# The last V pair of a cached-attention decode block, loaded in three pieces, its first piece partly by transfers of three partitions

## Chip, core and metric

One core of one Trainium2 chip runs the whole kernel. The metric is the device time of one execution in microseconds (us), lower is better. Before the change the median of three runs is 1293.55 us (1293.53 to 1293.67).

## What is computed

One decode step of a transformer block, in bf16: layer norm, attention of 4 sequences x 32 heads over a cache of 8192 keys and values, an output projection with residual, then a gated feed-forward part with its own layer norm and residual. The caches are 2 x 256 MiB, and each is read once.

```python
def _A_ref(x, k_cache, v_cache, wq, wo):          # x: [4, 1, 512], caches: [4, 32, 8192, 128]
    q = (x @ wq).reshape(B, Sq, H, Dh).transpose(0, 2, 1, 3)
    scores = jnp.einsum("bhqd,bhkd->bhqk", q, k_cache) * (Dh ** -0.5)
    p = _softmax(scores, axis=-1)
    o = jnp.einsum("bhqk,bhkd->bhqd", p, v_cache)
    return o.transpose(0, 2, 1, 3).reshape(B, Sq, H * Dh) @ wo
def _B_ref(x, w_gate, w_up, w_down):
    h = _sigmoid(x @ w_gate) * (x @ w_up)
    return h @ w_down
h  = x + _A_ref(_layernorm(x), k_cache, v_cache, wq, wo)
h2 = h + _B_ref(_layernorm(h), w_gate, w_up, w_down)
```

## The kernel before

The 128 (sequence, head) caches of K are handled in 64 pairs of heads, numbered n = 0 to 63, and those of V likewise. A pair is a tile of 128 partitions x 16384 bf16 values (32 KB in each partition, 4 MiB in all). It lies in one of the four slots of the SBUF tensor `KV`. Slots are handed out in rotation by `take_slot`; a transfer into a slot waits until the pair that held it before has been used up: a K pair by its last transpose on VectorE (line 380), a V pair by its last matmul (line 473).

All large transfers are issued by SyncE (SP) in one written order, `order` (line 333): the query weights, then K and V pairs alternately with K four pairs ahead, and at the end V60, V61, V62, V63, `wg`, `wu`, `wd` (gate, up and down weights, which go into slots of `KV` too). `wg` waits for the slot of V60, `wu` for that of V61, `wd` for that of V62. SP issues one after the other, so a transfer that waits for its slot holds back those behind it. A transfer over 128 partitions is carried by 16 DMA engines, each of which works through its rows in order of issue. `wd` comes as three transfers of 8, 4 and 2 of its 14 row blocks (`WDT`).

A pair is used in eight chunks of 4 KB per partition (`RC` x `DH` = 2048 values; `NCH` = 8). For V, `pv(u)` multiplies chunk m of pair n with the softmax weights in `PT`: four matmuls of 128x512 for each chunk. `t_v[n]` lists the completion tokens of the transfers that bring pair n, and `pv` waits for the one that covers its chunk. All V pairs come as one transfer, except the last one, V63: `emit_pair` cuts it into four transfers of two chunks each (1 MiB, 8 KB per partition; lines 297 to 301), with a semaphore each (`vl0` to `vl3`).

After the last chunk of V63 comes a chain of small steps: `finish` (copy to `O_sb`, selection matmuls of line 491, transposition of line 498, projection of line 507), the second layer norm (lines 207 to 225), the gate and up matmuls (line 596), the sigmoid (line 601), the product `hhT` (line 603), and the down matmuls (line 624), which need `hhT` and the three parts of `wd`. The cast of line 629 and the output transfer of line 630 end the kernel.

Of the kernel before, what the change touches and what calls it, by code (L numbers as in the profile page):

```python
# [11 lines left out]
NSL = 4  # L12
# [3 lines left out]
GH = 8  # L16
GP = 4
WDT = (0, 8, 12, 14)


class _Prog:
# [27 lines left out]
    def emit(self, eng, fn, waits=(), incs=1):  # L49

        todo = self._waits(eng, waits)
        tok = self.token(eng, incs) if incs else None

        def run(e):
            for key, v in todo:
                e.wait_ge(self.sems[key], v)
            made = fn(e)
            made = made if isinstance(made, list) else [made]
            if incs:
                assert len(made) == incs  # L60
                for m in made:
                    m.then_inc(self.sems[eng], 1)

        self.ops[eng].append(run)
        return tok
# [14 lines left out]
def bass_sequential_preLN__mha_block_cached__glu_gated_glu__decode_kernel(  # L80
# [13 lines left out]
    _, H, S, DH = A_k_cache.shape  # L94
# [5 lines left out]
    RC = 16  # L100
    NCH = R // RC
    NH = B * H
    NP = NH // 2
# [6 lines left out]
    prog = _Prog()  # L110
    emit = prog.emit

    with ExitStack() as es:
        def SB(name, shape, dt):
            return es.enter_context(nc.sbuf_tensor(name, shape, dt))
# [19 lines left out]
        KV = SB("KV", [128, NSL, R * 128], BF16)  # L135
# [28 lines left out]
        def in_slot(slot, inner, at=0):  # L164
            return bass.AP(raw(KV), slot * R * 128 + at, [[KVROW, 128], *inner])
# [10 lines left out]
        def obank(g):  # L176
            return bank[2 + g % 2]

        keys = ["sp", "act", "dve", "pool", "pe", "x", "out", "wg", "wu", "wd0", "wd1", "wd2", "wq", "wo"]
        keys += [f"sl{i}" for i in range(NSL)] + [f"k0p{i}" for i in range(4)] + [f"vl{i}" for i in range(4)]  # L180
        for k in keys:
            prog.sems[k] = es.enter_context(nc.semaphore("s_" + k))

# [3 lines left out]
            out=ident[:, :], in_=ident[:, :], compare_op=ALU.not_equal, fill=1.0, base=0,  # L187
# [3 lines left out]
            out=identf[:, :], in_=identf[:, :], compare_op=ALU.not_equal, fill=1.0, base=0,  # L191
# [74 lines left out]
        t_v = {}  # L266
# [4 lines left out]
        def kv_src(cache, n):  # L271
            b, h = n % GP, 2 * (n // GP)
            return cache[b, h:h + 2, :, :].rearrange("h (p r) d -> (h p) (r d)", p=64)
# [12 lines left out]
        def take_slot(job):  # L286
            i = n_alloc[0] % NSL
            w = freed(held_by[i])
            n_alloc[0] += 1
            held_by[i] = job  # L290
            slot_of[job] = i
            return i, w

        def emit_pair(kind, n, cache, done, pieces, cut):
            slot, w = take_slot((kind, n))
            src = kv_src(cache, n)
            if cut > 1:
                q = R * 128 // cut
                done[n] = [prog.dma("sp", f"{pieces}{s}", lambda e, s=s: e.dma_start(
                    KV[:, slot, q * s:q * (s + 1)], src[:, q * s:q * (s + 1)]), w) for s in range(cut)]  # L300
                return
            done[n] = [prog.dma("sp", f"sl{slot}", lambda e: e.dma_start(KV[:, slot, :], src), w)]

        def emit_weight(kind):
            slot, w = take_slot((kind, 0))
            if kind == "wd":
                wd_v = in_slot(slot, [[D, NFT], [1, D]])
                src = B_w_down.rearrange("(t p) f -> p t f", p=128)
                t_w[kind] = (wd_v, [prog.dma("sp", f"wd{i}", lambda e, i=i: e.dma_start(  # L309
                    wd_v[:, WDT[i]:WDT[i + 1], :], src[:, WDT[i]:WDT[i + 1], :]), w) for i in range(len(WDT) - 1)])  # L310
                return
            view = in_slot(slot, [[F, NDC], [1, F]])
            src = (B_w_gate if kind == "wg" else B_w_up).rearrange("(c p) f -> p c f", p=128)
            t_w[kind] = (view, prog.dma("sp", kind, lambda e: e.dma_start(view, src), w))

        def emit_wq():
            src = A_wq.rearrange("(p c) f -> p (c f)", p=128)
            t_wq.append(prog.dma("sp", "wq", lambda e: e.dma_start(Wreg[:, :], src)))
# [4 lines left out]
        def emit_wo():  # L323
            src = A_wo.rearrange("(g p e) f -> p g (e f)", p=128, e=4)
            dst = Wreg[:, :].rearrange("p (g f) -> p g f", g=NG // 2)
            t_wo.append(prog.dma("sp", "wo", lambda e: e.dma_start(dst, src), [t_qproj[0]]))  # L326
# [11 lines left out]
        def ready(kind, n):  # L338
            if kind == "wo":
                return bool(t_qproj)  # L340
            return kind == "wq" or freed(held_by[n_alloc[0] % NSL]) is not None

        def pump():
            while next_dma[0] < len(order) and ready(*order[next_dma[0]]):
                kind, n = order[next_dma[0]]
                next_dma[0] += 1
                if kind == "k":
                    emit_pair("k", n, A_k_cache, t_k, "k0p", 4 if n == 0 else 1)
                elif kind == "v":
                    emit_pair("v", n, A_v_cache, t_v, "vl", 4 if n == NP - 1 else 1)  # L350
                elif kind == "wq":
                    emit_wq()
                elif kind == "wo":
                    emit_wo()
                else:
                    emit_weight(kind)

        pump()


# [4 lines left out]
        t_ptc = {}  # L365
# [89 lines left out]
        def pv(u):  # L455
            n, m = u // NCH, u % NCH
            g, i = n // GP, n % GP
            first = i == 0 and m == 0
            last = i == GP - 1 and m == NCH - 1
            slot = slot_of["v", n]  # L460
            w = [t_v[n][m * len(t_v[n]) // NCH], t_ptc[g]]
            if first and g > 1:
                w.append(t_oev[g - 2])

            def f(e):
                mms = []
                for j in range(4):
                    k = 4 * m + j
                    o = k * 128 + i * 32
                    at = [[RC * 128, 4], [1, 128]], (64 * (k % 2) + k // 2) * 128  # L470
                    if n:
                        at = [[1, 512]], 512 * k
                    mms.append(e.matmul(obank(g)[32 * j:32 * (j + 1), :], PT[:, g % 2, o:o + 32], in_slot(slot, *at),  # L473
                                        start=first, stop=last, tile_position=(0, 32 * j)))
                return mms if last else mms[-1]
            tok = emit("pe", f, w, incs=4 if last else 1)
            if m == NCH - 1:
                t_pv[n] = tok
            if last:
                t_pvg[g] = tok  # L480
# [75 lines left out]

        q_projection()
        pump()
        for kind, n in steps:
            for m in range(NCH):  # L560
                u = NCH * n + m
                if kind == "k":
                    transposes(n, m)
                    advance()
                    scores(u)
                    if m == NCH - 1:
                        if n + NLQ < NP:
                            q_windows(n + NLQ)
                        if n % GP == GP - 1:
                            chain += [(tick[0] + d, fn) for d, fn in softmax(n // GP)]  # L570
                else:
                    advance()
                    pv(u)
                    if m == NCH - 1 and n % GP == GP - 1:
                        chain += [(tick[0] + d, fn) for d, fn in finish(n // GP)]
                pump()
# [10 lines left out]
        t_hn, _ = layernorm(sth, st_["h"], 1, hnT, bank[XS], st_["xs"])  # L587
# [30 lines left out]
        t_r = emit("pe", f_res, [t_res])  # L618
        for i in range(len(WDT) - 1):
            def f_down(e, i=i):  # L620
                mms = []
                for t in range(WDT[i], WDT[i + 1]):
                    for c in range(NDC):
                        mms.append(e.matmul(rows(c), hhT[:, t, :], wd_v[:, t, 128 * c:128 * (c + 1)],  # L624
                                            start=False, stop=(t == NFT - 1), tile_position=(0, 32 * c),
                                            skip_group_check=True))
                return mms[-4:]
# [5 lines left out]
        key, v = t_out  # L633
# [55 lines left out]
```

## Time and profile before

| what | value |
|---|---|
| median of three runs | 1293.55 us |
| the profiled execution's own time | 1293.53 us |
| its span, first to last instruction | 1291.7 us |
| TensorE matmul busy | 777.4 us (60%) |
| VectorE busy | 722.6 us (56%) |
| bytes read from HBM | 550.77 MB, 426 GB/s over the span |
| share of the ordinary DMA queue (q1) of 16 engines' span | 99.5% |
| mean granted TensorE clock | 0.790 |

The span leaves out 1.83 us of the profiled execution that lie before its first and after its last instruction. Matmul busy time is modelled at its end and says little of a limit; the DMA share is a mean over the 16 engines, so a share under 1 can mean that some of them have nothing left to do while others still work. A line of the timeline gives start and length of a group of instructions, the engine, the line of the program, the operation, the tiles it writes and reads, the number of instructions, and in brackets how long the engine had been idle before and what ended that.

### The profile page before, as it was taken

Reading aid. Unit: us, or ns where it says so; the run is one execution under the profiler, and the core shown is the slowest. Engines: PE = TensorE matmul, PEld = TensorE weight load, DVE = VectorE, ACT = ScalarE, POOL = GpSimd, SP = SyncE. Lnnn points to the kernel's source line nnn. Section 1 sums busy time; section 2 is a strip of 40 time slices with the busy share of each in tenths; the row PEclk is TensorE's granted clock in tenths of the full one; section 3 lists DMA queues with packets and bytes.
Section 4 is the critical chain, followed back from the end, with each engine's and each line's share of the span. In section 5 each row is a group of like instructions: output and inputs, shape, how many; then the busy total and the mean of one; then the engine's idle time right before and its main releaser. Section 6 shows DMA issues by size and latency. Waiting matters only on the chain.

```text
span 1291.7 us, 10570 instructions
## 1 busy us (share of the span) xinstructions
PE 777.4 (60%) x4768; PEld 308.4 (24%) x4768; DVE 722.6 (56%) x761; ACT 28.0 (2%) x56; POOL 10.9 (1%) x13
## 2 busy tenths in 40 slices
PE   4575656647557557556656657466465666566464
PEld 2222212213212222222222222122122222222122
DVE  5584745736555555645637556465645647456340
ACT  0000000000000000000000000000000000000001
POOL 3000000000000000000000000000000000000000
PEclk9788778877788687787788787787787886787775
DMA  9999999999999999999999999999999999999997
GB/s 396 430 432 428 435 428 434 429 431 431 433 431 428 433 431 432 428 433 432 432 430 431 432 430 434 427 435 429 430 435 426 435 428 433 434 425 437 425 433 305
DMA packets 23448, 551.45 MB, mean 427 GB/s; under 512 B 2280, under 2 KB 4076, under 8 KB 6124
## 3 DMA queue, kind: packets, MB, share of 16 engines
q1 hardware_dynamic: 23396, 550.78, 99.5%
q8 instruction: 37, 0.61, 0.2%
q14 instruction: 7, 0.06, 0.0%
q10 hardware_dynamic: 8, 0.00, 0.0%
HBM read 550.77 MB, written 0.00 MB: 426 GB/s over the span
## 4 chain that ended last, share of the span: by engine, by line
DMA 76%; DVE 21%; PE 1%; SPq 1%; issue 0%; ACT 0%
DMA KV<-in_A_k_cache_dram 72%; DVE kTc L380 21%; DMA KV<-in_A_v_cache_dram 2%; DMA Wreg<-in_A_wq_dram 1%; PE PS L399 1%; SPq L309 1%; DMA KV<-in_B_w_down_dram 1%; PE PS L521 0%; PE PS L473 0%; ACT E_sb L434 0%; DVE mpart L411 0%; PE PS L624 0%; PE PS L429 0%; SPq L326 0%; PE PS L440 0%
## 5 line engine op out<-in xcount | busy, mean ns | idle before, releaser
L399 PE MATMUL PS<-kTc,Lq 128*128 128x512 bf16 x2048 | 589.1, 446 | 450.7 <-DVE kTc L380 446.7
L380 DVE STREAM_TRANSPOSE kTc<-KV 128x1024 f32<-128x1024 f32 x512 | 586.8, 1209 | 371.2 <-DMA KV<-in_A_k_cache_dram 363.4
L399 PEld LDWEIGHTS PS<-kTc,Lq 128*128 128x128 bf16 x2048 | 210.0, 110 | 817.4 <-DVE kTc L380 545.9
L473 PE MATMUL PS<-KV,PT 128*32 128x512 bf16 x2048 | 138.0, 397 | 23.2 <-DMA KV<-in_A_v_cache_dram 14.3
L452 DVE STREAM_TRANSPOSE PT<-E_sb 64x512 bf16<-64x512 bf16 x32 | 78.4, 2450 | 1.0
L473 PEld LDWEIGHTS PS<-KV,PT 128*32 128x32 bf16 x2048 | 49.9, 99 | 85.5 <-issue 28.4
L545 DVE TENSOR_TENSOR Lq<-q,amask 128x16 bf16<-128x16 bf16 x64 | 14.2, 229 | 85.7 <-PE PS L399 85.6
L434 ACT ACTIVATE E_sb<-PS,negmb 128x512 bf16<-128x512 f32 x16 | 11.0, 687 | 1194.2 <-DVE negmb L432 1194.2
L491 PE MATMUL PS<-O_sb,pick 128*64 128x128 f32 x128 | 31.5, 428 | 0.8 <-ACT O_sb L483 0.8
L496 DVE CAST O_row<-PS 128x128 bf16<-128x128 f32 x8 | 2.3, 292 | 51.8 <-PE PS L491 51.8
L491 PEld LDWEIGHTS PS<-O_sb,pick 128*64 128x64 f32 x128 | 25.1, 224 | 13.8 <-issue 12.2
L416 PE MATMUL PS<-identf,mpart 128*1 128x128 f32 x32 | 6.1, 271 | 13.8 <-DVE mpart L411 13.8
L442 DVE RECIPROCAL rsum<-PS 128x1 f32<-128x1 f32 x16 | 2.7, 168 | 19.4 <-PE PS L440 19.3
L411 DVE TENSOR_REDUCE mpart<-PS 128x1 f32<-128x512 f32 x16 | 10.9, 684 | 2.1 <-PE PS L399 2.1
L579 POOL MEMSET kTc<- 128x448 bf16 x1 | 0.5, 471 | 1225.8 <-PE PS L399 1225.8
L483 ACT ACTIVATE O_sb<-PS 128x512 f32<-128x512 f32 x16 | 9.6, 597 | 53.8 <-PE PS L473 53.8
L521 PE MATMUL PS<-xnT,Wreg 128*128 128x4 bf16 x128 | 3.6, 166 | 8.6 <-DMA Wreg<-in_A_wq_dram 8.6
L440 PE MATMUL PS<-sig,Gmat 128*128 128x1 f32 x32 | 6.0, 257 | 4.5 <-ACT E_sb L434 4.5
L420 DVE TENSOR_REDUCE mrow<-PS 1x8 f32<-1x128 f32 x16 | 4.4, 276 | 7.1 <-PE PS L473 7.1
L429 PE MATMUL PS<-identf,rowpad 128*128 128x1 f32 x32 | 6.0, 257 | 2.8 <-DVE rowpad L424 2.8
L440 PEld LDWEIGHTS PS<-sig,Gmat 128*128 128x128 f32 x32 | 4.8, 187 | 12.1 <-ACT E_sb L434 11.9
L429 PEld LDWEIGHTS PS<-identf,rowpad 128*128 128x128 f32 x32 | 4.8, 187 | 10.4 <-DVE rowpad L424 10.3
(70 smaller groups left out, 75.8 us busy)
## 6 DMA issues: line engine op xcount, KB each, us to landing
KV<-in_A_k_cache_dram SPq DMA_DIRECT2D x63, 4096.0 KB, 29.7
KV<-in_A_v_cache_dram SPq DMA_DIRECT2D x63, 4096.0 KB, 34.9
Wreg<-in_A_wq_dram SPq DMA_DIRECT2D x1, 4096.0 KB, 12.2
KV<-in_A_k_cache_dram SPq DMA_DIRECT2D x4, 1024.0 KB, 17.9
Wreg<-in_A_wo_dram SPq DMA_DIRECT2D x1, 4096.0 KB, 27.4
KV<-in_A_v_cache_dram SPq DMA_DIRECT2D x4, 1024.0 KB, 28.9
KV<-in_B_w_gate_dram SPq DMA_DIRECT2D x1, 1792.0 KB, 28.2
KV<-in_B_w_up_dram SPq DMA_DIRECT2D x1, 1792.0 KB, 25.0
```

The costliest lines, as they stand in the source:

```text
L309: t_w[kind] = (wd_v, [prog.dma("sp", f"wd{i}", lambda e, i=i: e.dma_start(wd_v[:, WDT[i]:WDT[i + 1], :], src[:, WDT[i]:WDT[i + 1], :]), w) ...
L380: t_copy[u] = emit("dve", lambda e: e.transpose(kTc[:, u % NKT, :], chunk(n, slot, s)), [t_k[n][s * len(t_k[n]) // NCH], t_score.get(u - N ...
L399: ins = e.matmul(sbank(g), Lq[:, n % NLQ, ce, off:off + 128], k3[:, :, ce // 2, :, ce % 2], start=first and ce == 0, stop=last and ce == 3)
L411: t_mx = emit("dve", lambda e: e.tensor_reduce(mpart[:, :], sbank(g), AX.X, ALU.max), [t_score[GP * NCH * (g + 1) - 1], st_.get("p1")])
L429: t = emit("pe", lambda e: e.matmul(bank[XS][:, 128:129], rowpad[:, :], identf[:, 0:1], start=True, stop=True), [box["d2"], t_rp0])
L434: box["a2"] = emit("act", lambda e: e.activation(E_sb[:, :], sbank(g), ACT.Exp, bias=negmb[:, 0:1], scale=SCALE, accum_out=sig[:, 0:1]), [ ...
L440: t = emit("pe", lambda e: e.matmul(bank[XS][:, 130:131], Gmat[:, :], sig[:, 0:1], start=True, stop=True), [box["a2"], t_gm])
L452: t_ptc[g] = emit("dve", lambda e, z=z, dst=dst: e.transpose(dst, E_sb[64 * z:64 * z + 64, :]), w)
L473: mms.append(e.matmul(obank(g)[32 * j:32 * (j + 1), :], PT[:, g % 2, o:o + 32], in_slot(slot, *at), start=first, stop=last, tile_position= ...
L483: t_oev[g] = emit("act", lambda e: e.activation(O_sb[:, :], obank(g), ACT.Copy), [t_pvg[g], st_.get("sel")])
L491: ins = e.matmul(bank[XO][lo:lo + 64, 0:128], pick[:, q, :], O_sb[:, 128 * q:128 * (q + 1)], start=(q == 0), stop=(q == 3), tile_position= ...
L545: t_lq[n] = emit("dve", lambda e: e.tensor_tensor(dst, src, keep, ALU.mult), [st_["q"], t_lq0, t_am, t_score.get(NCH * (n - NLQ + 1) - 1)])
```

## The change

The last V pair, V63, comes in three pieces of 3, 3 and 2 chunks instead of four of 2 chunks. Pieces two and three are transfers over 128 partitions as before (12 KB and 8 KB per partition). The first piece (12 KB per partition) is split by partitions: partitions 48 to 127 come by one transfer of 80 rows on `vl0`, and partitions 0 to 47 by sixteen transfers of three rows each, all on a new semaphore `vh`. The matmuls of the first three chunks wait for both `vl0` and the last value of `vh`. Nineteen transfers are issued in place of four; the bytes are the same.

```diff
+LASTV = (0, 3, 6, 8)
+HEADP = 48
...
-        keys = ["sp", "act", "dve", "pool", "pe", "x", "out", "wg", "wu", "wd0", "wd1", "wd2", "wq", "wo"]
-        keys += [f"sl{i}" for i in range(NSL)] + [f"k0p{i}" for i in range(4)] + [f"vl{i}" for i in range(4)]
+        keys = ["sp", "act", "dve", "pool", "pe", "x", "out", "wg", "wu", "wd0", "wd1", "wd2", "wq", "wo", "vh"]
+        keys += [f"sl{i}" for i in range(NSL)] + [f"k0p{i}" for i in range(4)] + [f"vl{i}" for i in range(3)]
...
             slot, w = take_slot((kind, n))
             src = kv_src(cache, n)
+            if kind == "v" and n == NP - 1:
+                at = [RC * DH * m for m in LASTV]
+                t = [prog.dma("sp", "vl0", lambda e: e.dma_start(
+                    KV[HEADP:128, slot, 0:at[1]], src[HEADP:128, 0:at[1]]), w)]
+                for p in range(0, HEADP, 3):
+                    th = prog.dma("sp", "vh", lambda e, p=p: e.dma_start(
+                        KV[p:p + 3, slot, 0:at[1]], src[p:p + 3, 0:at[1]]))
+                t += [prog.dma("sp", f"vl{i}", lambda e, i=i: e.dma_start(
+                    KV[:, slot, at[i]:at[i + 1]], src[:, at[i]:at[i + 1]])) for i in (1, 2)]
+                done[n] = [[t[i]] + [th] * (i == 0) for i in range(3) for _ in range(LASTV[i], LASTV[i + 1])]
+                return
...
-                    emit_pair("v", n, A_v_cache, t_v, "vl", 4 if n == NP - 1 else 1)
+                    emit_pair("v", n, A_v_cache, t_v, "vl", 1)
...
-            w = [t_v[n][m * len(t_v[n]) // NCH], t_ptc[g]]
+            tv = t_v[n][m * len(t_v[n]) // NCH]
+            w = [*(tv if isinstance(tv, list) else [tv]), t_ptc[g]]
```

## Prediction

> **What bounds the kernel now.** I read the DMA queues first, then the windows of the tail (engine busy times, granted clock, DMA share, GB/s), then its timeline.
>
> ```profile
> DMA packets 23448, 551.45 MB, mean 427 GB/s; under 512 B 2280, under 2 KB 4076, under 8 KB 6124
> ...
> q1 hardware_dynamic: 23396, 550.78, 99.5%
> q8 instruction: 37, 0.61, 0.2%
> ...
> q10 hardware_dynamic: 8, 0.00, 0.0%
> ```
>
> The 16 DMA engines have q1 work for 99.5% of the span, so bytes set the pace up to the tail. The counts also tell how many engines carry a transfer. On q10 there is only x, four rows; 8 packets are four rows and four semaphore increments, so four engines. On q1, 141 transfers over 128 partitions make 21,120 rows and 141 x 16 increments, and the output 16 rows and 4 increments: 21,120 + 2,256 + 20 = 23,396. So a transfer of few rows does not use 16 engines, and one of three rows uses, as I read it, three.
>
> ```profile
> 1266.00:1275.00 9.00, 4.95 (x52) 1.35 (x48) 0.00 (x0) 0.00 (x0) 0.00 (x0) 0.69 1.01 410
> 1275.00:1278.00 3.00, 2.22 (x15) 1.37 (x8) 0.00 (x0) 1.99 (x3) 0.00 (x0) 0.50 1.04 384
> 1278.00:1281.00 3.00, 1.49 (x21) 1.01 (x19) 1.22 (x6) 0.09 (x1) 0.00 (x0) 0.50 0.64 243
> ```
>
> The share falls to 0.64 while weights are outstanding: a third of the engines wait. The trace's semaphore increments (one from each engine of a transfer) give the order: V62 is finished by seven engines at 1256.6 to 1257.3 us, by six at 1262.9 to 1263.3, by three at 1264.5 to 1264.8; the last piece of V63 by the same groups at 1266.6 to 1267.3, 1272.9 to 1273.2 and 1274.4 to 1274.8. Seven engines lead by 6 to 8 us, and a piece is complete only with its last engine. The trace doesn't tell the engines' numbers.
>
> ```profile
> 1241.47 1.75 SPq L299 DMA_DIRECT2D KV<-in_A_v_cache_dram  x4
> ...
> 1251.01 0.38 SPq L314 DMA_DIRECT2D KV<-in_B_w_gate_dram  x1
> ...
> 1274.81 1.04 PE L473 MATMUL PS<-KV,PT 128*32 128x512 bf16 x8 [1.89 <-DMA KV<-in_A_v_cache_dram]
> ...
> 1285.86 0.40 DVE L603 TENSOR_TENSOR kTc<-sg_sb,PS 128x56 bf16<-128x56 f32 x1 [3.31 <-PE PS L596]
> ...
> 1288.05 1.08 PE L624 MATMUL PS<-KV,kTc 128*32 128x128 bf16 x24 [0.36 <-DMA KV<-in_B_w_down_dram]
> ...
> 1289.26 0.29 DVE L629 CAST o_sb<-PS 128x128 bf16<-128x128 f32 x1 [3.00 <-PE PS L624]
> 1289.58 0.69 SPq L630 DMA_DIRECT2D out_dram<-o_sb  x1
> ```
>
> Two paths end together. The last V63 matmuls start at 1274.81 when the last engine delivers; 11.45 us of small steps follow to the end of `hhT` at 1286.26. On the DMA side the last engine goes on with `wg`, `wu`, `wd` for 13.92 us, to 1288.68, and the last down matmuls wait for it. Both begin where the latest engine leaves V63: **the end moves by as much as that moment moves.**
>
> **The change part by part.** Rows of 32 KB take 1.213 us in the packet records and rows of 8 KB 0.312; linearly, one of 12 KB takes 0.46.
>
> *Bytes by engine.* Before, each engine brings 32 rows of 8 KB of V63: 9.98 us. After, the 80-row part gives it five rows of 12 KB (2.30), piece two eight (3.68), piece three eight of 8 KB (2.50): 8.48, that is 1.50 less. Three engines have 16 rows of 12 KB more, 7.36, and are 5.86 later than before, if all sixteen transfers use the same three.
>
> *Three engines side by side.* [...] Bounds for the 48 rows: 7.36 us if the three don't hinder each other, 48 x 0.46 = 22.1 if together they are no faster than one. The nearest row is x, whose 1 KB packets go into partitions 0 to 3: three started within 0.03 us and were over in 0.133, three times the 0.044 of the quick ones, which speaks for the upper end; but two of them took 0.044 at the same time, which speaks for the lower. Between the two I take the middle, 14.7 us. On leading engines V63 then ends at 1257.0 + 2.30 + 14.7 + 3.68 + 2.50 = 1280.2, against 1274.8: **+5.4 us.** With the bounds it is -1.5 (the others set the end then) and +12.8.
>
> [...]
>
> [...]
>
> *Issue on SP.* Four transfers took 1.75 us, 0.44 each, and the four-engine output 0.69. Nineteen cost 8.4 to 12.4 us, so SP is free at 1249.8 to 1253.8 rather than 1243.2. Behind them waits `wg`, which may be issued from 1251.01: at most 2.8 us late. No engine reaches its rows before 1266.6, so that hides it; without that cover it would be 2.8. `wu` waits for V61's matmuls until 1258.72 and isn't delayed. Pieces two and three are in the queue before the first engine needs them (1256.6 + 2.3). I take 0. The three issues of `wd` occupy SP for 13.17 us from 1268.48, and parts two and three land behind the latest engine's rows; V63 has 21 rows on most engines instead of 32, so I expect no later issue. Bounds: 0, or the gain of a good case kept back in full.
>
> *Matmuls and waits.* The groups are 12, 12 and 8 matmuls instead of four of 8 (0.85 us); the last is unchanged. Twelve take 1.3 us and pieces arrive 2.5 to 3.7 us apart, so they hide. The new wait for `vh` stands before V63's first matmuls; only V63's others and `finish` are queued behind it on TensorE, and they need that data anyway. One wait more costs 0.
>
> **Sum.** The profiled execution took 1293.53 us (span 1291.7 and 1.83 around it), as good as the median of 1293.55. 1293.5 + 5.4 = **1298.9 us**, slower.
>
> **Rivals.**
>
> *A, it balances.* The three engines are of the seven leading ones and don't hinder each other: they end V63 at 1267.26 + 5.86 = 1273.1, the latest of the others at 1274.76 - 1.50 = 1273.3. Everything behind moves by -1.5: 1292.0, or up to 1293.5 if `wd` doesn't follow. For it: the lead is there, and 5.86 just fits in it; two packets of x were undisturbed. Against: it needs the right three engines and free neighbours. This is the case not slower than before; it holds in full while the 48 rows take up to 7.5 us, and turns slower than before when they take over 9.0 (1274.76 - 1267.26 + 1.50).
>
> *C, late engines.* The three belong to the nine others. Then even unhindered V63 ends at 1273.2 + 5.86 = 1279.1 (+4.3) or 1274.76 + 5.86 = 1280.6 (+5.9): 1297.9 to 1299.4, the same figure as my forecast for another reason. Nine of 16 engines are late, so a blind draw of three would meet one more often than not; against it, x's rows were served at 1.67 to 1.70 us on three engines and at 2.27 on the fourth, and three engines finish their first rows of `wq` clearly before the rest and stay among the leaders: I take these, without proof, for engines of x.
>
> *D, both:* late and hindered, 1274.76 - 1.5 + 14.7 = 1288.0, +13.2: 1306.7.
>
> *E, it doesn't do what it says:* the transfers go to ever other engines, and each has five and three rows, eight as before: 1293.5.
>
> **How the numbers follow.** The forecast has 0.38 (own range 1295.2 to 1302.6, a hindrance of 1.5 to 2.5 times), A 0.36, C 0.13, D 0.05, E 0.05; 0.03 is left for a gain over 0.2% (2.6 us, about what a measurement of this kernel can tell from no change), for which I see no mechanism. Slower: 0.38 + 0.13 + 0.05 = 0.56; same: A and E, 0.41. The range reaches from A to the forecast's upper end, 1291.8 to 1303.0; D, part of the forecast's tail and the unexplained gain are left out.
>
> **What would show it.** In the profile after, the first matmuls of V63 start late (about 1274 in the forecast, about 1267 to 1270 in A), the last group about 1280.2 (A: 1273.3; C: 1279 to 1281). The packets of the 48 rows take well over 0.46 us in the forecast, 0.46 in A and C. SP's nineteen issues last 8 to 12 us. V63's last piece is finished late by three engines alone in the forecast and C; in A by the same groups as now, closer together. `wg`'s issue at 1251 to 1254, and the distance from the last V matmuls to the cast of line 629 (14.4 us), stay. The forecast is wrong if the rows keep 0.46 us on leading engines.

## The result, and the profile after

| | before | changed |
|---|---|---|
| median of six runs each | 1293.6 us (1293.44 to 1293.67) | 1301.72 us (1301.16 to 1302.91) |
| the profiled execution's own time | 1293.53 us | 1302.91 us |
| its span | 1291.7 us | 1301.1 us |
| start of the last matmuls of V63 | 1274.81 | 1284.17 |
| start of the cast before the output | 1289.26 | 1298.64 |

The change makes the kernel 8.1 us slower: ratio 1.0064, 95% interval 1.0053 to 1.0075. The two profiled executions lie 9.4 us apart, and the last V63 matmuls as well.

The DMA queues after:

```profile
DMA packets 23352, 551.45 MB, mean 424 GB/s; under 512 B 2312, under 2 KB 4108, under 8 KB 6156
...
q1 hardware_dynamic: 23300, 550.78, 99.5%
```

The bytes are the same, and there are 96 packets fewer on q1. V63 had 512 rows and 4 x 16 = 64 semaphore increments; now it has 80 + 48 + 128 + 128 = 384 rows, 48 increments of the three wide transfers and, for the difference to come out, 48 of the sixteen small ones: three each, so three engines each.

The first window of the tail before (the next ones stand in the prediction; busy times, granted clock, DMA share, GB/s), and the start of V62's matmuls before:

```profile
1256.00:1266.00 10.00, 3.85 (x40) 1.15 (x36) 0.00 (x0) 0.00 (x0) 0.00 (x0) 0.50 0.97 410
...
1264.83 4.46 PE L473 MATMUL PS<-KV,PT 128*32 128x512 bf16 x40 [6.16 <-DMA KV<-in_A_v_cache_dram]
```

The windows of the tail after, with the same columns:

```profile
1256.00:1266.00 10.00, 2.29 (x24) 0.58 (x16) 0.00 (x0) 0.00 (x0) 0.00 (x0) 0.50 1.04 253
1266.00:1275.00 9.00, 3.47 (x32) 1.09 (x32) 0.00 (x0) 0.00 (x0) 0.00 (x0) 0.50 0.96 176
1275.00:1278.00 3.00, 0.14 (x4) 0.00 (x0) 0.00 (x0) 0.00 (x0) 0.00 (x0) 0.50 0.98 281
1278.00:1281.00 3.00, 1.47 (x12) 0.34 (x12) 0.00 (x0) 0.00 (x0) 0.00 (x0) 0.50 0.98 403
```

Here the lost time is seen whole. The 16 DMA engines are as busy as ever (share 0.96 to 1.04), but they move 253 and then 176 GB/s, where they moved 410 in both of the first two windows before. This is not waiting for work: packets are under way, and most take longer. The trace's packet records say how much: a 12 KB row, 0.46 us undisturbed, takes 0.89 in the median and 1.39 at most, about twice and three times that. Rows of V62 (32 KB, 1.213 us) are caught too, with up to 3.04 us.

The issues and the V matmuls in the timeline after:

```profile
1241.10 0.34 SPq L301 DMA_DIRECT2D KV<-in_A_v_cache_dram  x1
...
1241.49 5.03 SPq L304 DMA_DIRECT2D KV<-in_A_v_cache_dram  x16
...
1246.56 0.83 SPq L306 DMA_DIRECT2D KV<-in_A_v_cache_dram  x2
...
1250.57 0.38 SPq L327 DMA_DIRECT2D KV<-in_B_w_gate_dram  x1
...
1271.53 3.60 PE L487 MATMUL PS<-KV,PT 128*32 128x512 bf16 x32 [13.24 <-DMA KV<-in_A_v_cache_dram]
...
1278.29 1.47 PE L487 MATMUL PS<-KV,PT 128*32 128x512 bf16 x12 [3.16 <-DMA KV<-in_A_v_cache_dram]
1281.65 1.47 PE L487 MATMUL PS<-KV,PT 128*32 128x512 bf16 x12 [1.88 <-DMA KV<-in_A_v_cache_dram]
1284.17 1.04 PE L487 MATMUL PS<-KV,PT 128*32 128x512 bf16 x8 [1.05 <-DMA KV<-in_A_v_cache_dram]
...
1298.64 0.29 DVE L643 CAST o_sb<-PS 128x128 bf16<-128x128 f32 x1 [3.03 <-PE PS L638]
```

The nineteen issues take 6.3 us and delay nothing: `wg` is issued at 1250.57. The first late thing is not V63 but V62: its matmuls start at 1271.53, after 13.24 us of waiting, where they started at 1264.83 before, although V62 is loaded by an unchanged transfer. V63 then follows at 1278.29, 1281.65 and 1284.17. From there to the cast it is 14.47 us, as before (14.45).

### The profile page after: what moved, and what is told of

Same layout as the page of the kernel before. It is cut to its first block, busy times and chain, and to the rows that moved or that the text cites. A ratio compares the mean times of both kernels' runs of the same rounds, so it can differ in the third digit from the quotient of the medians.

```text
span 1301.1 us, 10586 instructions
## 1 busy us (share of the span) xinstructions
PE 781.9 (60%) x4768; PEld 310.2 (24%) x4768; DVE 722.7 (56%) x761; ACT 28.0 (2%) x56; POOL 10.9 (1%) x13
## 4 chain that ended last, share of the span: by engine, by line
DMA 76%; DVE 21%; PE 1%; SPq 1%; issue 0%; ACT 0%
DMA KV<-in_A_k_cache_dram 72%; DVE kTc L393 21%; DMA KV<-in_A_v_cache_dram 2%; DMA Wreg<-in_A_wq_dram 1%; PE PS L412 1%; SPq L322 1%; DMA KV<-in_B_w_down_dram 1%; SPq L304 0%; PE PS L535 0%; PE PS L487 0%; ACT E_sb L447 0%; DVE mpart L424 0%; PE PS L638 0%; PE PS L442 0%; SPq L339 0%
```

## Experiments

The theories: **P**, engines that write into the same group of neighbouring partitions slow each other down, whichever engines they are; **T**, what costs is the pile of extra rows on three engines; **N**, the number of transfers; **H**, rows that lie side by side in HBM. That an engine brings the same partitions in every transfer over 128 of them is assumed in some of the expectations; no trace tells an engine's partitions. Each time stands beside 1293.57 to 1293.67 us for the kernel before, run on the same chips.

**The cut into three pieces alone.**

```diff
-                t = [prog.dma("sp", "vl0", ...KV[HEADP:128...]...)]
-                for p in range(0, HEADP, 3): ...
-                t += [... for i in (1, 2)]
-                done[n] = ...
+                t = [prog.dma("sp", f"vl{i}", lambda e, i=i: e.dma_start(
+                    KV[:, slot, at[i]:at[i + 1]], src[:, at[i]:at[i + 1]]), w) for i in range(3)]
+                done[n] = [t[i] for i in range(3) for _ in range(LASTV[i], LASTV[i + 1])]
```

> V63 in three transfers over all 128 partitions (3, 3 and 2 chunks); no split by partitions. Every theory holds the cut into three for harmless, because each engine has the same bytes for the same partitions: 1293.5 us within 0.2, last matmuls of V63 at 1274.8. If it is over 1295, the sizes of the pieces matter and not their split by partitions.

1293.5 us, ratio 0.9999 (0.999 to 1.0008). The 12 KB packets take 0.46 to 0.47 us. The pieces cost nothing; all of the loss is in the split by partitions.

**The 48 rows in one transfer.**

```diff
-                for p in range(0, HEADP, 3):
-                    th = prog.dma("sp", "vh", lambda e, p=p: e.dma_start(
-                        KV[p:p + 3, slot, 0:at[1]], src[p:p + 3, 0:at[1]]))
+                th = prog.dma("sp", "vh", lambda e: e.dma_start(
+                    KV[0:HEADP, slot, 0:at[1]], src[0:HEADP, 0:at[1]]))
```

> As the changed kernel, but partitions 0 to 47 come by one transfer of 48 rows (three rows for each of 16 engines, 16 semaphore increments) in place of sixteen transfers of three rows. No engine has more bytes than another. Theory P (what hurts is that engines write into the same groups of neighbouring partitions, whichever engines they are): still slow, since rows no longer go to the engine that usually brings them: 1297 to 1301 us, 12 KB rows stretched from 0.46 to 0.9 us or more. Theory T (what hurts is the pile of 16 rows on three engines): 1293.5. Theory N (what hurts is the number of transfers): 1293.5 to 1294.

1304.45 us, ratio 1.0082 (1.0067 to 1.0097): slower than the change, and more than P's range had. Median of the 12 KB packets 0.89 us, as in the change, but at most 1.79. With four transfers instead of nineteen and, if the 48 rows go to 16 engines as expected, no pile on three, T and N do not explain the loss.

**Three rows four partitions apart.**

```diff
-                for p in range(0, HEADP, 3):
+                for p in [12 * j + s for j in range(HEADP // 12) for s in range(4)]:
...
-                        KV[p:p + 3, slot, 0:at[1]], src[p:p + 3, 0:at[1]]))
+                        KV[p:p + 9:4, slot, 0:at[1]], src[p:p + 9:4, 0:at[1]]))
```

> As the changed kernel, but the three rows of each of the sixteen transfers are partitions p, p+4, p+8 instead of p, p+1, p+2; same engines, bytes and number. Theory P: the three no longer meet each other, but still meet the engines that are bringing V62 and the 80 rows: 2 to 3 us better than the change, 1297 to 1300. Theory T and theory N: as the change, 1301 to 1303. Theory H (what hurts is three engines reading side by side in HBM): back to 1293.5 or better, as the rows read are now 128 KB apart.

1300.38 us, ratio 1.0052 (1.0035 to 1.0069), 1.3 us better than the change, where P had 2 to 3, and just above P's range. Keeping the three engines apart from each other thus gives back the smaller part; that the rest is lost to meetings with other engines is my reading. The increments of `vh` in the trace speak for it: the first four transfers, into partitions 0 to 11, end some 0.5 us apart (1261.95, 1262.51, 1262.99, 1263.51), nearly a row's undisturbed time, and the other twelve, into partitions 12 to 47, 0.94 us apart on average (the last at 1274.78). All are written four apart, so the distance alone does not free them. That the first four go where the three engines write anyway, and the other twelve where others do, is how I read it; it was not shown. H's return to 1293.5 did not come.

**The same three-row transfers in addition to the kernel before, three ways.** Here V63 stays in its four pieces, and sixteen transfers of three rows bring rows of V63 a second time, into parts of SBUF that nothing reads any more.

```diff
+                        own = [z + s for z in (0, 32) for s in range(4)]
+                        side = list(range(0, 24, 3))
+                        for to, width in zip(spare, (6144, 4096)):
+                            for d, f in zip(side, side):
+                                prog.dma("sp", "ex", ... to[d:d + 3, :], src[f:f + 3, 0:width] ...)
```

> The kernel before, with V63 in its four pieces, and after its first piece sixteen additional transfers of three rows into spare parts of SBUF that nothing reads (eight of 12 KB and eight of 8 KB rows, partitions p, p+1, p+2 for p = 0, 3, ... 21). Three engines have 6.2 us more to move (8 x 0.46 + 8 x 0.31), which fits into a lead of 6 to 8 us if they are leading ones. Theory P: rows stretched to two or three times their time, V63 delayed by 4 to 10 us: 1298 to 1303. Theory T: three engines with more rows, but within the lead: about 1293.5. Theory H: slow as well, as the rows read are side by side too.

1297.74 us, ratio 1.0031 (1.0019 to 1.0043), just under P's range. The second way has the same reads and writes to partitions four apart, from 0 to 11 and from 32 to 43. That the three engines bring these partitions anyway was my assumption; it was not shown:

```diff
-                            for d, f in zip(side, side):
-                                prog.dma("sp", "ex", ... to[d:d + 3, :], src[f:f + 3, 0:width] ...)
+                            for d, f in zip(own, side):
+                                prog.dma("sp", "ex", ... to[d:d + 9:4, :], src[f:f + 3, 0:width] ...)
```

> As the run with additional transfers side by side, with the same sizes, number and rows read from HBM (side by side), but written to partitions p, p+4, p+8 with p = 0 to 3 and 32 to 35. [...] Theory H: as slow as side by side. Theory N: as slow as side by side.

1293.48 us, ratio 0.9999 (0.9989 to 1.0008). The third writes side by side as the first and reads rows that are four apart:

```diff
-                            for d, f in zip(side, side):
-                                prog.dma("sp", "ex", ... to[d:d + 3, :], src[f:f + 3, 0:width] ...)
+                            for d, f in zip(side, own):
+                                prog.dma("sp", "ex", ... to[d:d + 3, :], src[f:f + 9:4, 0:width] ...)
```

> As the run with additional transfers side by side, written to partitions p, p+1, p+2, but the rows read from HBM are four rows (128 KB) apart. Theory P: unchanged against side by side, 1298 to 1303. Theory H: back to 1293.5.

1297.82 us, ratio 1.0033 (1.0019 to 1.0046), again just under P's range. These three decide between the theories. The windows of the first (written side by side):

```profile
1256.00:1266.00 10.00, 1.81 (x20) 0.40 (x12) 0.00 (x0) 0.00 (x0) 0.00 (x0) 0.67 0.99 313
1266.00:1275.00 9.00, 5.70 (x48) 1.36 (x48) 0.00 (x0) 0.00 (x0) 0.00 (x0) 0.50 1.00 340
```

of the second (written four apart):

```profile
1256.00:1266.00 10.00, 3.62 (x40) 1.17 (x36) 0.00 (x0) 0.00 (x0) 0.00 (x0) 0.67 0.97 409
1266.00:1275.00 9.00, 4.72 (x52) 1.27 (x48) 0.00 (x0) 0.00 (x0) 0.00 (x0) 0.69 1.00 410
```

and of the third (written side by side, read apart):

```profile
1256.00:1266.00 10.00, 2.31 (x24) 0.61 (x16) 0.00 (x0) 0.00 (x0) 0.00 (x0) 0.50 0.99 303
1266.00:1275.00 9.00, 5.49 (x48) 1.36 (x48) 0.00 (x0) 0.00 (x0) 0.00 (x0) 0.50 1.01 342
```

All keep the engines busy; only the second keeps the rate, 409 and 410 GB/s against 410 and 410 before. Its 24 rows of 12 KB take 0.46 to 0.47 us each; written side by side they take 0.82 in the median and up to 1.21, read apart 0.93 and up to 1.25. So it follows where the rows are written, as P has it; the distance in HBM, 32 or 128 KB, makes no difference (1297.74 and 1297.82 us), and H is out. T and N are out as well: in the second run sixteen more transfers on the same three engines cost nothing. The second run shows two more things. Its three engines had 6.2 us more to move and the time didn't change, so they are leading ones: of the seven that finished the last piece of V63 at 1266.6 to 1267.3 before, four are left there (1266.6 to 1267.6), and the other twelve increments come from 1272.8 to 1274.6. And the rows of these transfers were not stretched: their 12 KB and 8 KB packets took at most 0.47 and 0.32 us. The run changes the distance and the set of partitions together; that the set is what counts is my reading of the transfers into partitions 0 to 11 and 12 to 47 above.

**The two halves of the split, each in addition to the kernel before** (again into spare SBUF): the sixteen transfers of 48 rows without the cut at partition 48, the 80 rows without the small transfers, and, as a measure for these, the same bytes over all 128 partitions.

```diff
+        for p in range(0, 48, 3):
+            prog.dma("sp", "ex", ... spare[p:p + 3, :], src[p:p + 3, 0:6144] ...)
```

> The kernel before, with V63 in its four pieces over 128 partitions, and the change's sixteen transfers of three rows of 12 KB (partitions 0 to 47) in addition, into spare SBUF that nothing reads; there is no cut at partition 48. If the three-row transfers alone made the change slower, this costs at least as much as the change: about 1302. If the transfer of 80 rows was part of it, less: 1297 to 1300, though 0.59 MB more are read.

1300.22 us, ratio 1.0051 (1.0036 to 1.0066), 6.6 us more: just above the range, but less than the change's 8.1, so the 80 rows have their part.

```diff
+        prog.dma("sp", "ex", ... spare[48:128, :], src[48:128, 0:6144] ...)
```

> The kernel before, and after V63's first piece one transfer of 80 rows of 12 KB (partitions 48 to 127) in addition into spare SBUF; no transfer of three rows. Five rows for each engine are 2.3 us. If the cut at partition 48 is harmless: 1293.6 + 2.3 = 1295.9. By theory P, five rows for each of 16 engines cannot all be the partitions that the engine usually brings (eight rows each), so rows meet: 12 KB packets at 0.6 to 0.9 us, 1297 to 1300.

1302.07 us, ratio 1.0064 (1.0047 to 1.0081), 8.5 us more and above P's range; median of the 12 KB packets 0.92 us.

```diff
+        prog.dma("sp", "ex", ... spare[:, 0:3840], src[:, 0:3840] ...)
```

> The same additional bytes as with the 80 rows (0.98 MB), but as one transfer over all 128 partitions with 7.5 KB rows: eight rows of about 0.29 us for each engine, 2.3 us, each engine in its own partitions. Every theory: 1295.9 within 0.4, packets not stretched. It is the measure for the 80 rows.

1295.85 us, ratio 1.0018 (1.0008 to 1.0027): 2.2 us for 0.98 MB more, the rate of the engines and nothing else. The last V matmuls of the run with 80 rows and of this one:

```profile
1279.10 1.04 PE L479 MATMUL PS<-KV,PT 128*32 128x512 bf16 x8 [5.61 <-DMA KV<-in_A_v_cache_dram]
1281.57 1.04 PE L479 MATMUL PS<-KV,PT 128*32 128x512 bf16 x8 [1.43 <-DMA KV<-in_A_v_cache_dram]
1284.11 1.04 PE L479 MATMUL PS<-KV,PT 128*32 128x512 bf16 x8 [1.49 <-DMA KV<-in_A_v_cache_dram]
```

```profile
1271.92 0.65 PE L479 MATMUL PS<-KV,PT 128*32 128x512 bf16 x8 [2.87 <-DMA KV<-in_A_v_cache_dram]
1274.41 1.05 PE L479 MATMUL PS<-KV,PT 128*32 128x512 bf16 x8 [1.84 <-DMA KV<-in_A_v_cache_dram]
1276.90 1.04 PE L479 MATMUL PS<-KV,PT 128*32 128x512 bf16 x8 [1.44 <-DMA KV<-in_A_v_cache_dram]
```

Both bring the same 0.98 MB more, 2.3 us of plain work for every engine; the one that is cut at partition 48 is 1302.07 - 1295.85 = 6.2 us dearer. So either half of the split is enough to make the kernel slower, the wide one too, which the prediction had at 2.3 us of plain work. The two (6.6 and 6.2 us) don't simply add up to the change's 8.1; that the same engines wait in both would explain it, but was not tested.

## Why the prediction was right, and what was mis-sized

The direction was right, and the reason was right in kind: engines hinder each other where they write neighbouring partitions (the additional 12 KB rows took 0.82 us in the median side by side, and 0.46 to 0.47 us four apart in partitions 0 to 11 and 32 to 43). But the forecast saw three engines that hinder each other, and most of the loss is elsewhere, as I read it between leading engines and those whose partitions they write; writing the rows of the three four partitions apart gave back only 1.3 of the 8.1 us. The time of 1298.9 us was 2.8 us short of the median, inside the range. That it came so near with the terms below left out is in part luck.

*Three engines for three rows* held (48 increments), and so did the belief that they are leading ones: the additional transfers four apart were free. So C, late engines, is out, and D with it; E, ever other engines, is out since exactly three of the seven leading engines lose their lead, both there and in the change.

*A, it balances*, had the right engines and the right lead; of the transfers of three rows only the additional ones into partitions 0 to 11 and 32 to 43 kept the undisturbed time in every row (0.46 to 0.47 us for 12 KB), and there nothing is moved off the late engines. In the change the condition "48 rows in up to 7.5 us" failed: the 48 increments of `vh` come from 1262.27 to 1278.16, some 16 us.

*The step that was mis-sized* is "on leading engines V63 then ends at 1257.0 + 2.30 + 14.7 + 3.68 + 2.50 = 1280.2, against 1274.8: +5.4 us". It let the hindrance fall on the three engines and their 48 rows alone. The 80-row part, 2.30, took the seven leading engines from 1256.7 - 1258.1 (V62's end) to 1261.3 - 1262.6, 4.5 to 4.7 us; the 48 rows then took some 16.6 instead of 14.7. Together that is 21.2 us from 1257.0 to 1278.16 instead of 17.0. Pieces two and three then took 5.96, as said (6.18). The remainder, 1284.1 less 1280.2, is these 4 us, more than half of them in the 80-row part. (These times are of the profiled execution, which took 9.4 us more than that of before; the median took 8.1 more.) That the wide transfer would be hindered was bounded nowhere, and the experiment with 80 rows shows it to be no smaller than the other half.

*What the leading engines do to the others* had no term either: the nine late engines end V62 at 1267.5 to 1271.5 instead of 1262.9 to 1264.8, though it is loaded as before; that they share their partitions with engines that have run ahead is how I read their stretched rows. So V63's last piece is not finished late by three engines alone, as the prediction had it: four increments come at 1273.3 to 1274.7, nine at 1281.3 to 1282.7, and three, which I take for those of the three engines, at 1283.1, 1283.6 and 1284.1. The nine alone would have put the end some 8 us late (1282.7 against 1274.8). The 1.50 us by which these nine were to be relieved were never seen.

*The rest.* The nineteen issues took 6.3 us, less than the 8.4 to 12.4, and delayed nothing, which is what was charged; `wg` was issued at 1250.57, before the 1251 to 1254 of the forecast. V63's first matmuls started at 1278.29 where about 1274 was forecast, which is the same error of 4 us. The tail behind V63 kept its length to 0.02 us, so both paths moved with V63, as said. The matmul groups and the wait for `vh` cost nothing: V63's first group waits 3.16 us for data that is late anyhow.

*The rows.* The forecast's 14.7 us gives the 48 rows twice their undisturbed time (7.36). In the change 55 of the 256 packets of 12 KB took less than 0.5 us, the median was 0.89 and the longest 1.39, so about once to three times 0.46. They do not confirm the 14.7 us, since these packets are those of all engines and not of the three alone.

## What to carry over

Here the lead of some DMA engines was spare bandwidth only for additional rows into partitions 0 to 11 and 32 to 43 (12 KB rows at 0.46 to 0.47 us, 1293.48 us in all). One engine writes 27 GB/s here (32 KB in 1.213 us), and with the split by partitions 12 KB rows took about two to three times as long (0.89 us in the median, 1.39 at most, instead of 0.46), so this split, which gave other engines' rows to three that were ahead, cost 8.1 us. How large a group of partitions is in which engines hinder each other was not measured, nor which engine brings which partition. In a tail like this one split a transfer by columns, over all 128 partitions (1293.5 us in three pieces), and not by partitions (1301.72 us); if a split by partitions is needed, read from the packet records whether its rows, and those of the transfers beside it, are stretched. And read the DMA share beside GB/s: here a share near 1 at 176 to 253 instead of 410 GB/s meant stretched rows, and a share of 0.64 (before, from 1278 to 1281 us) meant missing work.

## What the runs showed of the hardware

- Additional data was free or had its plain price: 0.49 MB more on three leading engines, into partitions 0 to 11 and 32 to 43, changed nothing (1293.48 us), and 0.98 MB over all engines cost 2.2 us.
- One transfer of 48 rows was worse than sixteen of three rows on three engines, each beside the 80-row part (1304.45 against 1301.72 us).
- Issuing a three-row transfer took SP 0.31 us with neighbouring rows (16 in 5.03 us), and 0.70 us with rows four partitions apart (16 in 11.13 us). Rows read four apart in HBM but written side by side stayed at 0.31 (8 in 2.53 us).
- The lead of the seven engines builds up over the whole run: in the kernel before, the 16 increments of a transfer over all partitions come within 0.6 us at 12 us, 2.4 at 256, 3.6 at 489, 5.0 at 839 and 8.1 at 1247, as nine engines fall back in steps of about 1.5 us. What holds these nine back was not tested.

Open: which engine brings which of the 80 rows, and so why that half costs as much as it does, was not measured. No experiment gave a version faster than both kernels; the best, three pieces over all partitions, is the same as before. Relief of the late engines by moving their rows at a time when nothing else is written into those partitions was not tried; I see no such time in this tail.
